# Batch 2 transposed in tile 0's second half, its global rows gathered by SyncE, its values loaded in fp32, and two key casts on ScalarE

## The chip, the cores and the metric

The kernel runs on one core of one Trainium2 chip. The metric is the device time of one execution in microseconds (us). Nine runs of the kernel before have a median of 350.7 us and lie between 349.97 and 352.67 us.

## What is computed

The reference is a sparse attention followed by a two-layer feed-forward stage. Cut to what matters:

```python
# q, k, v: 8 batches x 8 heads x 576 positions x 64, fp32; global_idx: 8 positions
scores = scale * np.matmul(q, k.transpose(0, 1, 3, 2))
mask = np.abs(pos[:, None] - pos[None, :]) <= 32
mask = mask | is_global[:, None] | is_global[None, :]
attn = softmax of scores where mask, else -1e9
x = (attn @ v).transpose(0, 2, 1, 3).reshape(4608, 512)
h = x @ w_in                                   # w_in 512 x 2048
g = np.maximum(h, 0.0) + np.log1p(np.exp(-np.abs(h)))
out = g @ w_out                                # w_out 2048 x 512
```

A query sees keys at most 32 positions away and the 8 global positions, and a global query sees everything.

## The kernel before

**The stages.** Batch 0's attention runs first, alone. Then come nine feed-forward tiles of 512 tokens, and the attention of batches 1 to 7 is threaded between their matmuls. A tile `n` has 16 slots. Slot `s` holds four matmuls of the first layer for tile `n` (`mm1`, L516 to L534), then the steps filed under `(16n+s, 0)`, then four matmuls of the second layer for tile `n-1` (`mm2`, L548, none in tile 0), then the steps filed under `(16n+s, 1)`. Each step is put there by `at(slot, half, function, arguments)` (L582), and `attend` (L666) calls what is filed. Nothing reorders the work afterwards: each engine runs its instructions in the order in which the program names them, and waits where an operand is not ready. Slots set only this order, not times, so an engine with little to do runs ahead of the slot that TensorE is in.

**Attention of one batch and one pair of heads.** Keys and queries must lie with the head dimension on the partitions. Batches 0 to 2 load runs of six positions (`load_runs`, L101), cast keys on an engine (`cast_runs`, L174), and turn both with TensorE transposes (`transposes`, L324) into a PSUM bank; `spread_columns` (L359) copies the bank into `KT` or `QT`. Batches 3 to 7 instead load whole token tiles (`load_tokens`), cast them on GpSimd (`cast_tokens`, L131), and are turned by a DMA transpose on SyncE's queue (`turn`, L135). Then `scores` makes two groups of products (L380) and their exponentials on ScalarE (L403), `mask` multiplies them by the band on VectorE (L412), `sums` and `values` multiply by ones and by the values (L434), `inv_ln` and `inv_exp` form the reciprocal on ScalarE (L456, L460), and `scale_x` writes the result into `xT` on VectorE (L472, L474). `glob_norm` and `glob_out` (L484, L490) do the global queries; `glob_out` is eight small GpSimd copies into `xT`. The first `mm1` of tile `n` waits for the batches that its tokens belong to.

**Columns of the global positions.** Batches 0 and 1 take them with six extra one-hot matmuls in `transposes` (L345). Batch 2 takes them in one go with `columns_of_2` (L496), 24 one-hot matmuls each for keys and queries, filed in slots 14 and 15 of tile 0. For batches 3 to 7, GpSimd issues 16 DMAs (`gather_rows`, L167), eight rows for keys and eight for queries, cast to bf16 on the way, in slots 18 to 25; `global_columns` (L504) transposes them in slot 27, and `spread_globals` (L142) copies them into each batch's tile.

**Batch 2 before.** Its transposes lie in tile 1: a key transpose of pair `p` at half slots 33, 39, 45, 51 and a query transpose half a slot later. GpSimd casts its keys and moves its queries into the key layout (`cast_runs` at slots 8 and 9), and loads its values with casting DMAs into `V1` (`load_v_cast`, L155, slot 12).

**PSUM.** During batch 0 and tile 0 one pool, `start_psum`, is open: two banks under tag `h`, which `mm1` alternates between, and three two-bank regions under tag `at`, handed out in turn to scores, sums, values and some transposes. At tile 1 this pool is closed and a second one opens over the same eight banks (L762 to L764): two banks `h`, one `o`, one `tp`, two regions `at`. The output of `mm2` takes `o`, and from its tile 1 on it alternates between `o` and `tp` (L554).

**Queues.** SyncE issues the loads of keys, of values and of batches 3 to 7, the DMA transposes and the stores; GpSimd issues the loads of queries, the weights and the gathers of rows. The loads of keys share the buffer `kq_f`, those of values share `v_f`, so a load waits for the casts of the one before. The framework numbers the DMAs of each of the two kinds over eight completion semaphores in turn: a DMA waits for the one eight places before it to have landed.

Of the kernel before, what the change touches and what calls it, by code (L numbers as in the profile page):

```python
# [19 lines left out]
P = 128  # L20
WIN = 32
KW = 120
NG = 8
# [17 lines left out]
def kernel(  # L41
# [43 lines left out]
    GB = B - 3  # L85
    glob_2 = {n: const.tile([P, NP, NG], BF16, name=f"{n}_g2") for n in "kq"}
# [31 lines left out]
    def tokens(n, b):  # L118
        if (n, b) not in tok:
            fresh = b < 5  # L120
            tok[n, b] = work.tile([P, NP * NTL * P], BF16, tag=f"{n}b", bufs=2, name=f"{n}t") if fresh else tok[n, b - 2]
            if fresh:
                nc.gpsimd.memset(tok[n, b][96:P], 0.0)  # L123
        return tok[n, b][:].rearrange("p (a t c) -> p a t c", a=NP, t=NTL)
# [17 lines left out]
    def spread_globals(n, b):  # L142
        dst = turned[n, b]
# [10 lines left out]

    def load_v_cast(b):  # L155
        o = V1[b % 2]
        nc.gpsimd.dma_start(out=o[KW:P], in_=v_rows[:, (b - 1) * HD:b * HD].unsqueeze(1).to_broadcast([NG, NTL, HD]))
        for t in range(NTL):
            nc.gpsimd.dma_start(out=o[:ST[t], t].rearrange("p (h d) -> p h d", d=D),  # L159
                                in_=v[b, :, KW * t:KW * t + ST[t], :].rearrange("h s d -> s h d"))  # L160

    def gather_v(g):
        nc.gpsimd.dma_start(out=v_rows[g:g + 1].rearrange("o (c d) -> c o d", d=D),
                            in_=v.rearrange("b h s d -> (b h) s d")[H:, bass.ds(positions[g], 1), :])


    def gather_rows(n, g):  # L167
        o = (hot_v[:].rearrange("p t c -> p (t c)") if n == "k" else VG[:])[g * GB:(g + 1) * GB, 0:HD]
        nc.gpsimd.dma_start(out=o.rearrange("p (h d) -> p h d", d=D).unsqueeze(2),
                            in_=src[n][B - GB:B, :, bass.ds(positions[g], 1), :])  # L170
# [68 lines left out]
    positions = []  # L239

    def load_positions():
        positions.extend(nc.values_load_multi_w_load_instructions(
            idx_r[0:1, :], engines=[mybir.EngineType.Pool], min_val=0, max_val=S - 1,
            skip_runtime_bounds_check_because="positions of the sequence")[1])
# [79 lines left out]
    def transposes(n, b, p, copy=nc.vector.tensor_copy, unread=0):  # L324

        parts = [(slice(0, P), lambda r: kqb[n, b][:, r, p * P:(p + 1) * P])]
        if n == "q" and b < 2:
            parts = [(slice(64 * e, 64 * e + 64), lambda r, e=e: raw[b][:, 2 * p + e, r * D:(r + 1) * D]) for e in range(2)]
        if b == 1 and p:
# [17 lines left out]
        else:  # L347
            copy = nc.vector.tensor_copy
            g = glob_2[n][:, p]
        spread = lambda: spread_columns(n, b, p, tb, g, copy)  # L350
        if b == 1 and p:
# [7 lines left out]
    def spread_columns(n, b, p, tb, g, copy):  # L359
# [5 lines left out]
        cg = copy if b < 2 else nc.gpsimd.tensor_copy  # L365
        if n == "k":
            cg(dst[:, p, :, KW:P], g.unsqueeze(1).to_broadcast([P, NTL, NG]))
        else:
            cg(dst[:, p, 0:4, KW:P], g.unsqueeze(1).to_broadcast([P, 4, NG]))
            cg(dst[:, p, 4, ST[4]:ST[4] + NG], g)  # L370
# [119 lines left out]
    def glob_out(b):  # L490
        xg = XG.pop(b)
        for g in range(NG):
            nc.gpsimd.tensor_copy(xT[:, :, b * S:(b + 1) * S][:, :, bass.ds(positions[g], 1)], xg[:, :, g:g + 1])  # L493


    def columns_of_2(n):  # L496
        ps = region("tp")
        for p in range(NP):
            for r in range(RUN):
                nc.tensor.matmul(out=ps[:, p * NG:(p + 1) * NG], lhsT=kqb[n, 2][:, r, p * P:(p + 1) * P],  # L500
                                 rhs=onehot[:NQ, r, :], start=(r == 0), stop=(r == RUN - 1))
        nc.vector.tensor_copy(glob_2[n][:].rearrange("p a g -> p (a g)"), ps[:, 0:NP * NG])

    def global_columns(n):  # L504
        rows = hot_v[:].rearrange("p t c -> p (t c)") if n == "k" else VG[:]
        ps = bank()
        tb = ps[:].bitcast(BF16)
        for p in range(NP):
            nc.tensor.transpose(out=tb[:, p * GB * NG:(p + 1) * GB * NG], in_=rows[:GB * NG, p * P:(p + 1) * P],
# [38 lines left out]
    def mm2(n, s):  # L548
        i, part = s // 4, s % 4
        if part == 0:  # L550


            last = n == n_tiles - 1
            ops[n] = psum["pool"].tile([P, d_model], FP32, tag="h" if last else "tp" if n and i % 2 else "o",  # L554
# [38 lines left out]
    for c in range(4):  # L593
        at(0, 0, load_w_out, c)
    for p in range(NP):
        for n in "kq":
            at(8 + p // 2, 0, cast_runs, n, 2, pair_heads(p), nc.gpsimd.tensor_copy)
    at(12, 0, load_v_cast, 2)
    for i, n in enumerate("kq"):
        at(14 + i, 0, columns_of_2, n)  # L600
        at(27, i, global_columns, n)
        for g in range(NG):
            at(18 + g, 0, gather_rows, n, g)

    def loads(b):
        s0 = STARTS[4 * b - 8] // 2
        if b == 3:
            k0, kt, q0, qt, v0 = s0 - 12, s0 - 7, s0 - 8, s0 - 3, s0 - 5
        elif b == 4:
            k0, kt, q0, qt, v0 = s0 - 15, s0 - 10, s0 - 11, s0 - 6, s0 - 8  # L610
        else:
            k0, kt, q0, qt, v0 = s0 - 23, s0 - 15, s0 - 16, s0 - 8, s0 - 9
        for n, first, last in (("k", k0, kt), ("q", q0, qt), ("v", v0, None)):
# [9 lines left out]
            else:  # L623
                at(last, 0, turn, n, b)
                at(max(last + 2, 28), 0, spread_globals, n, b)

    for b in range(1, B):
# [8 lines left out]
        for p in range(NP):  # L636
# [8 lines left out]
            if (b, p) != (1, 0):  # L645
                if b < 3:
                    step(to_transposes, transposes, "k", b, p)
                    step(to_transposes + (b > 1), transposes, "q", b, p)
# [9 lines left out]
            step(to_inverse, inv_exp, p)  # L658
            step(to_x, scale_x, b, p)
        step(to_x + (b > 1), glob_norm, b)  # L660
# [22 lines left out]
    load_positions()  # L683
# [6 lines left out]
    cast_runs("k", 0, pair_heads(2), nc.gpsimd.tensor_copy)  # L690
    build_mask_0(nc.vector)
    build_bias(0)
    cast_runs("k", 0, pair_heads(3), nc.gpsimd.tensor_copy)
# [8 lines left out]
    for i in range(NP):  # L702
        load_runs("k", 1, pair_heads(i))
    for grp in range(2):
        products(0, 0, grp)
    exponentials(0, 0, 0)
    transposes("k", 0, 1, unread=2)
# [95 lines left out]
```

The softmax here doesn't subtract the row's maximum and nothing guards it: scores larger than these inputs give would overflow.

## Time and profile before

| what | value |
|---|---|
| median of nine runs | 350.7 us |
| the profiled execution: time, span | 351.84 us, 350.2 us |
| TensorE busy (its matmuls) | 334.0 us, 95% of the span |
| ScalarE, VectorE, GpSimd busy | 270.3, 135.2, 128.1 us |
| clock granted to TensorE | 1.0 throughout |
| DMA, of which on SyncE's queue and on GpSimd's | 47.34 MB; 40.09 MB and 6.80 MB |

The span is what the hardware profiler saw from first to last instruction of the execution; 1.64 us of the measured time lie around it. In the page, each group of instructions has a line with its source line, engine, operation, output and inputs, count, busy time and mean duration, then the idle time of the engine just before and what ended it. L521 is `mm1`, L540 `mm2`. From the timeline: tile 0 begins at 31.66 us, its slot 10 at 54.03 us, tile 1 at 62.23 us, tile 2 at 106.75 us.

### The profile page before, as it was taken

Reading aid. Unit: us, or ns where it says so; the run is one execution under the profiler, and the core shown is the slowest. Engines: PE = TensorE matmul, PEld = TensorE weight load, DVE = VectorE, ACT = ScalarE, POOL = GpSimd, SP = SyncE. Lnnn points to the kernel's source line nnn. Section 1 sums busy time; section 2 is a strip of 40 time slices with the busy share of each in tenths; the row PEclk is TensorE's granted clock in tenths of the full one; section 3 lists DMA queues with packets and bytes.
Section 4 is the critical chain, followed back from the end, with each engine's and each line's share of the span. In section 5 each row is a group of like instructions: output and inputs, shape, how many; then the busy total and the mean of one; then the engine's idle time right before and its main releaser. Section 6 shows DMA issues by size and latency. Waiting matters only on the chain.

```text
span 350.2 us, 7185 instructions
## 1 busy us (share of the span) xinstructions
PE 334.0 (95%) x2757; PEld 162.8 (46%) x2757; DVE 135.2 (39%) x397; ACT 270.3 (77%) x425; POOL 128.1 (37%) x265
## 2 busy tenths in 40 slices
PE   7898898999799999999999999999999999999996
PEld 3555444444344444444444444444444444444444
DVE  7863362265543344333444443334333100100021
ACT  3677899788778988888888888888888777777700
POOL 7954648996476336315432451402000100000000
PEclk9999999999999999999999999999999999999999
DMA  7999999999996999999899888700000100010012
GB/s 168 212 231 210 206 188 195 179 149 199 170 214 141 167 196 177 220 188 223 184 180 185 175 187 154 127 32 30 32 30 32 62 30 32 30 60 32 30 60 90
DMA packets 128169, 47.34 MB, mean 135 GB/s; under 512 B 114288, under 2 KB 123416, under 8 KB 128136
## 3 DMA queue, kind: packets, MB, share of 16 engines
q1 hardware_dynamic: 113752, 40.09, 57.8%
q0 software_dynamic: 14240, 6.80, 14.6%
q8 instruction: 21, 0.34, 0.4%
q14 instruction: 12, 0.10, 0.1%
q10 hardware_dynamic: 144, 0.01, 0.0%
HBM read 37.56 MB, written 9.55 MB: 135 GB/s over the span
## 4 chain that ended last, share of the span: by engine, by line
PE 71%; DMA 10%; POOL 7%; issue 4%; ACT 2%; DVE 2%; SPq 1%; POOLq 0%; ACTq 0%
PE o L540 31%; PE hp L521 30%; PE av L434 5%; PE sc L392 3%; DMA kq_f<-in_k_dram 3%; DMA v_f<-in_v_dram 2%; DMA q_raw<-in_q_dram 2%; DMA hot_v<-in_k_dram 2%; DMA kq_f<-in_q_dram 1%; POOL kt L123 1%; SPq L140 1%; POOL kt L132 1%; ACT ex L403 1%; POOL V L159 1%; PE sc L385 1%
## 5 line engine op out<-in xcount | busy, mean ns | idle before, releaser
L521 PE MATMUL hp<-xT,w_in_t 128*128 128x512 bf16 x576 | 147.6, 380 | 2.7 <-POOL xT L493 1.4
L540 PE MATMUL o<-w_out_t,gt 128*128 128x512 bf16 (+1 forms) x592 | 145.3, 373 | 0.7 <-DVE ot L545 0.7
L533 ACT ACTIVATE e<-hp 128x512 f32<-128x512 f32 x128 | 76.2, 595 | 37.9 <-PE hp L521 36.5
L540 PEld LDWEIGHTS <-gt 128*128 128x128 bf16 x592 | 57.1, 98 | 66.0 <-issue 2.0
L534 ACT ACTIVATE gt<-e 128x512 bf16<-128x512 f32 x128 | 80.6, 630 | 4.1
L521 PEld LDWEIGHTS <-w_in_t 128*128 128x128 bf16 x576 | 52.2, 98 | 65.5 <-issue 5.8
L545 DVE COPY ot<-o 128x512 f32<-128x512 f32 (+1 forms) x37 | 24.9, 672 | 66.5 <-PE o L540 66.5
L403 ACT ACTIVATE ex<-sc 128x1008 bf16<-128x1008 f32 (+1 forms) x56 | 48.6, 919 | 1.7 <-PE sc L392 1.1
L412 DVE TENSOR_TENSOR ex<-ex,mask 128x1008 bf16<-128x1008 bf16 (+1 forms) x48 | 32.6, 684 | 20.9 <-ACT ex L403 19.8
L444 DVE TENSOR_REDUCE gs<-av 128x8 f32<-128x32 f32 x64 | 12.0, 187 | 60.9 <-ACT rz L456 57.5
L493 POOL COPY xT<-xg 128x4 bf16 x64 | 15.4, 241 | 54.4 <-DVE xg L488 51.0
L182 POOL CAST V<-v_f 128x512 bf16<-128x512 f32 (+3 forms) x45 | 23.2, 536 | 29.6 <-DMA v_f<-in_v_dram 23.9
L472 DVE TENSOR_TENSOR xT<-av,rz 128x480 bf16<-128x480 f32 x28 | 18.4, 657 | 37.2 <-ACT rz L460 37.0
L132 POOL CAST kt<-kq_f 120x512 bf16<-120x512 f32 (+1 forms) x25 | 16.2, 659 | 20.0 <-DMA kq_f<-in_k_dram 19.7
L456 ACT ACTIVATE rz<-av 128x616 f32<-128x616 f32 x28 | 19.0, 680 | 4.6 <-PE av L434 2.5
L132 POOL CAST qt<-kq_f 120x512 bf16<-120x512 f32 (+1 forms) x25 | 15.9, 645 | 14.8 <-DMA kq_f<-in_q_dram 14.7
L460 ACT ACTIVATE rz<-rz 128x616 f32<-128x616 f32 x28 | 19.7, 703 | 0.2
L434 PEld LDWEIGHTS <-ones 128*64 128x64 bf16 x384 | 12.5, 109 | 11.6 <-issue 11.2
L434 PE MATMUL av<-ex,ones 128*64 128x160 bf16 (+1 forms) x336 | 16.7, 233 | 0.8 <-DVE ex L412 0.8
L434 PE MATMUL av<-ex,V 128*64 128x160 bf16 (+1 forms) x336 | 16.2, 229 | 1.2 <-POOL V L182 1.2
L392 PE MATMUL sc<-QT,KT 64*128 64x200 bf16 (+2 forms) x200 | 13.4, 242 | 1.9 <-DVE xT L474 1.0
L434 PEld LDWEIGHTS <-V 128*64 128x64 bf16 x384 | 13.7, 110 | 2.2 <-POOL V L182 1.5
(137 smaller groups left out, 238.9 us busy)
## 6 DMA issues: line engine op xcount, KB each, us to landing
out_dram<-ot SPq DMA_DIRECT2D x35, 256.0 KB, 2.2
v_f<-in_v_dram SPq DMA_DIRECT2D x24, 240.0 KB, 6.3
kq_f<-in_k_dram SPq DMA_DIRECT2D x20, 240.0 KB, 5.1
kq_f<-in_q_dram SPq DMA_DIRECT2D x20, 240.0 KB, 4.8
kq_f<-in_k_dram SPq DMA_DIRECT2D x12, 288.0 KB, 8.5
w_in_t<-in_moe_w_in_dram POOLq DMA_DIRECT2D x4, 512.0 KB, 7.6
w_out_t<-in_moe_w_out_dram POOLq DMA_DIRECT2D x4, 512.0 KB, 16.0
v_f<-in_v_dram SPq DMA_DIRECT2D x6, 192.0 KB, 4.1
```

Source lines behind the costliest of these rows:

```text
L132: nc.gpsimd.tensor_copy(tokens(n, b)[:ST[t], :, t, :], kq_f[:ST[t], t * HD:(t + 1) * HD].rearrange("p (a c) -> p a c", a=NP))
L182: eng.tensor_copy(V1[b % 2][:rows, t, cols], v_f[:rows, t, cols])
L392: nc.tensor.matmul(out=sc[:, e, GOFF[t]:GOFF[t] + w], lhsT=kT[r, p, t, :], rhs=qT[r, p].rearrange("p t c -> p (t c)")[:, WLO[t]:WHI[t]], s ...
L403: nc.scalar.activation(out=ex, in_=sc[:, :, 0:GW[grp]], func=ACTF.Exp, scale=SCALE)
L412: nc.vector.tensor_tensor(out=ex, in0=ex, in1=masks[grp][:, 0:GW[grp]].unsqueeze(1).to_broadcast([P, 2, GW[grp]]), op=ALU.mult)
L434: nc.tensor.matmul(out=av[64 * e:64 * e + 64, OFF + lo:OFF + hi], lhsT=weight(t, e), rhs=exps[p, grp][rows, e, c:c + hi - lo], start=(firs ...
L460: nc.scalar.activation(out=RZ[p], in_=RZ[p], func=ACTF.Exp, scale=-1.0)
L521: nc.tensor.matmul(out=hp[:], lhsT=w_in_t[:, kd, kf * P:(kf + 1) * P], rhs=xT[:, kd, n * NT:(n + 1) * NT], start=(kd == 0), stop=(kd == KD ...
L533: nc.scalar.activation(out=e[:], in_=hp[:], func=ACTF.Exp)
L534: nc.scalar.activation(out=gts[n][:, kf, :], in_=e[:], func=ACTF.Ln, bias=1.0)
L540: nc.tensor.matmul(out=op, lhsT=gts[n][:, kf, i * P:(i + 1) * P], rhs=w_out_t[:, kf, cols], start=(kf == 0), stop=(kf == KF - 1))
L545: nc.vector.tensor_copy(ot[:, cols], op)
```

## The change

- **Batch 2's transposes** move from tile 1 to half slots 21, 24, 27 and 30 of tile 0. Keys and queries of a pair go together into one two-bank region. The queries are taken from their raw layout, twelve transposes of 64 columns instead of six of 128. The four moves of queries into the key layout are gone.
- **Global rows** are gathered for batches 2 to 7, by SyncE, in fp32, into two buffers that tile 0 does not use, and cast to bf16 by GpSimd in slot 6. `columns_of_2` and the small GpSimd copies of batch 2's columns are gone; `global_columns` runs in slot 10, `spread_globals` for batch 2 in slot 15. SyncE loads the eight positions into registers as well.
- **Batch 2's values** are loaded in fp32 on SyncE's queue (slot 9) and cast by GpSimd (slots 12 to 14).
- **Key casts of batch 0**, pairs 2 and 3, go from GpSimd to ScalarE, and the loads of batch 1's keys are named after them.
- **Batches 3 and 4** get fixed slots, mostly two slots earlier than before. The zeroing of their four token tiles goes from GpSimd to VectorE.
- **The second PSUM pool** has two single banks `o0` and `o1` for the output in place of `o` and `tp`.
- **`glob_norm`** of batch 0 and of batch 1 comes before the last `scale_x` instead of after it.

The diff, cut to its core:

```diff
-    GB = B - 3
-    glob_2 = {n: const.tile([P, NP, NG], BF16, name=f"{n}_g2") for n in "kq"}
+    GB = B - 2
...
             if fresh:
-                nc.gpsimd.memset(tok[n, b][96:P], 0.0)
+                nc.vector.memset(tok[n, b][96:P], 0.0)
...
     def gather_rows(n, g):
-        o = (hot_v[:].rearrange("p t c -> p (t c)") if n == "k" else VG[:])[g * GB:(g + 1) * GB, 0:HD]
-        nc.gpsimd.dma_start(out=o.rearrange("p (h d) -> p h d", d=D).unsqueeze(2),
-                            in_=src[n][B - GB:B, :, bass.ds(positions[g], 1), :])
+        if n not in g_f:
+            g_f[n] = work.tile([P, NT], FP32, tag="e", bufs=2, name="g_f")
+        nc.sync.dma_start(out=g_f[n][g * GB:(g + 1) * GB, 0:HD].rearrange("p (h d) -> p h d", d=D).unsqueeze(2),
+                          in_=src[n][B - GB:B, :, bass.ds(positions[SP][g], 1), :])
+
+    def global_rows(n):
+        return (hot_v[:].rearrange("p t c -> p (t c)") if n == "k" else VG[:])[:GB * NG, 0:HD]
+
+    def cast_rows(n):
+        nc.gpsimd.tensor_copy(global_rows(n), g_f[n][:GB * NG, 0:HD])
...
-        if n == "q" and b < 2:
+        if n == "q":
             parts = [(slice(64 * e, 64 * e + 64), lambda r, e=e: raw[b][:, 2 * p + e, r * D:(r + 1) * D]) for e in range(2)]
-        if b == 1 and p:
+        if (b, p) > (1, 0):
             if n == "k":
                 both[p] = region("tp")
...
-            ops[n] = psum["pool"].tile([P, d_model], FP32, tag="h" if last else "tp" if n and i % 2 else "o",
+            ops[n] = psum["pool"].tile([P, d_model], FP32, tag="h" if last else f"o{i % 2}",
...
-    for p in range(NP):
-        for n in "kq":
-            at(8 + p // 2, 0, cast_runs, n, 2, pair_heads(p), nc.gpsimd.tensor_copy)
-    at(12, 0, load_v_cast, 2)
-    for i, n in enumerate("kq"):
-        at(14 + i, 0, columns_of_2, n)
-        at(27, i, global_columns, n)
-        for g in range(NG):
-            at(18 + g, 0, gather_rows, n, g)
+    at(0, 0, load_positions, SP)
+    for i, n in enumerate("kq"):
+        for g in range(NG):
+            at(1 + 2 * i + g // 4, 0, gather_rows, n, g)
+        at(6, 0, cast_rows, n)
+        at(10, i, global_columns, n)
+        at(15, 1, spread_globals, n, 2)
+    for p in range(NP):
+        at(8, 0, cast_runs, "k", 2, pair_heads(p), nc.gpsimd.tensor_copy)
+        for n in "kq":
+            at((21 + 3 * p) // 2, (21 + 3 * p) % 2, transposes, n, 2, p)
+    at(9, 1, load_v_rows, 2)
+    at(9, 1, load_v, 2)
+    for t in range(NTL):
+        at(12 + t // 2, 0, cast_v, 2, t, nc.gpsimd)
...
-        if b == 3:
-            k0, kt, q0, qt, v0 = s0 - 12, s0 - 7, s0 - 8, s0 - 3, s0 - 5
-        elif b == 4:
-            k0, kt, q0, qt, v0 = s0 - 15, s0 - 10, s0 - 11, s0 - 6, s0 - 8
+        if b < 5:
+            k0, kt, q0, qt, v0 = ((14, 19, 18, 23, 22), (24, 29, 28, 33, 33))[b - 3]
...
-                at(max(last + 2, 28), 0, spread_globals, n, b)
+                at(first, 0, tokens, n, b)
+                at(last + 2, 0, spread_globals, n, b)
...
-                if b < 3:
+                if b < 2:
                     step(to_transposes, transposes, "k", b, p)
-                    step(to_transposes + (b > 1), transposes, "q", b, p)
+                    step(to_transposes, transposes, "q", b, p)
...
+            if (b, p) == (1, NP - 1):
+                step(to_x, glob_norm, b)
             step(to_x, scale_x, b, p)
-        step(to_x + (b > 1), glob_norm, b)
+        if b > 1:
+            step(to_x + 1, glob_norm, b)
...
-    cast_runs("k", 0, pair_heads(2), nc.gpsimd.tensor_copy)
     build_mask_0(nc.vector)
     build_bias(0)
-    cast_runs("k", 0, pair_heads(3), nc.gpsimd.tensor_copy)
...
     exponentials(0, 0, 0)
+    cast_runs("k", 0, pair_heads(2), act_copy)
...
     scores(0, 1, 0)
+    cast_runs("k", 0, pair_heads(3), act_copy)
+    for i in range(NP):
+        load_runs("k", 1, pair_heads(i))
...
-            psum.update(pool=ctx.enter_context(tc.tile_pool(name="psum", bufs=1, space=PSUM)), bank="tp", banks=1, at=2)
+            psum.update(pool=ctx.enter_context(tc.tile_pool(name="psum", bufs=1, space=PSUM)), at=2)
```

## The prediction

> **What bounds the kernel now.** I read the busy time by stretches first (columns: the stretch, its length, then busy us of TensorE's matmuls, its weight loads, VectorE, ScalarE and GpSimd, granted clock, DMA share, GB/s).
>
> ```profile
> 40.00:60.00 20.00, 18.73 (x240) 9.69 (x240) 8.27 (x36) 19.01 (x27) 13.29 (x26) 1.00 1.20 191
> 60.00:80.00 20.00, 18.66 (x188) 9.79 (x186) 8.91 (x22) 15.48 (x24) 19.79 (x31) 1.00 1.34 169
> 80.00:100.00 20.00, 17.45 (x167) 8.83 (x164) 10.52 (x32) 14.68 (x23) 11.25 (x25) 1.00 1.14 188
> ...
> 140.00:160.00 20.00, 20.00 (x154) 9.27 (x152) 8.01 (x21) 18.00 (x30) 5.92 (x11) 1.00 1.08 208
> ```
>
> From 140 us on TensorE has no idle time, so the end is what TensorE does plus its idle time before 140. Only the first 140 us can give or take. In tile 0 (31.66 to 62.23) ScalarE is nearly full; from 60 to 80 GpSimd is.
>
> Next the waits of TensorE's matmuls from 0 to 140 us (total us, times, longest):
>
> ```profile
> PE sc L392 <- DVE xT L474: 1.8, 3, 0.8
> ...
> PE hp L521 <- POOL xT L493: 1.4, 2, 0.8
> PE tp L509 <- DMA hot_v<-in_k_dram: 1.3, 1, 1.3
> PE av L434 <- POOL V L182: 1.2, 2, 0.7
> PE hp L521 <- ACT first_rz L527: 1.0, 2, 0.8
> PE av L434 <- DVE ex L412: 0.8, 2, 0.4
> PE o L540 <- DVE ot L545: 0.7, 1, 0.7
> ...
> PE hp L521 <- DVE q_g L502: 0.4, 1, 0.4
> ```
>
> The 14 waits add up to some 12 us. Those between 62 and 107 us (tile 1) are the three on `scale_x`, one on the mask, the gathered rows, the output copy, and 0.75 on `glob_out`.
>
> Last the timeline of tile 0's end: TensorE, ScalarE and VectorE.
>
> ```profile
> 54.03 1.90 PE L521 MATMUL hp<-xT,w_in_t 128*128 128x512 bf16 x8
> ...
> 56.71 1.89 PE L521 MATMUL hp<-xT,w_in_t 128*128 128x512 bf16 x8 [0.79 <-ACT first_rz L527]
> 58.78 1.02 PE L521 MATMUL hp<-xT,w_in_t 128*128 128x512 bf16 x4 [0.18 <-ACT first_rz L527]
> ...
> 61.10 0.75 PE L500 MATMUL tp<-onehot,qb 96*128 96x8 bf16 x24
> 62.23 0.59 PE L521 MATMUL hp<-xT,w_in_t 128*128 128x512 bf16 x2 [0.38 <-DVE q_g L502]
> ```
>
> ScalarE holds TensorE up by about 1 us there: the slack into which the transposes are put. The last row matters most: the first matmul of tile 1 waits for the copy of `q_g`, no operand of it. It is the first tile of the second PSUM pool, and waits until everything of the first has been read.
>
> **The Trainium skill.** "DMA: Bandwidth & Descriptors", section "SWDGE vs HWDGE vs iDMA": a DMA can cast only when GpSimd issues it. So moving loads to SyncE adds casts. The trace agrees: SyncE loads are fp32 with casts behind them. The same section has all DMAs share the same 16 engines, so a changed queue moves no byte away; the DMA share is above 0.9 until 120 us. "VectorE: DVE Perf Modes", section "Zero memsets can be issued as uint32 (trn2)": a zeroing of bf16 on VectorE can count half the elements. It agrees: 32x2560 bf16 took 2.23 us on GpSimd (L123), and the same size as 32x1280 uint32 1.12 us on VectorE (L209).
>
> **The change part by part.**
>
> *Before slot 10 of tile 0 (54.03 us).* The two key casts (0.83 us each on ScalarE) fall into its waits for TensorE, at 9.7 to 10.6 and 13.9 to 15.1; GpSimd's freed 1.6 us are mostly lost again, since its last `gather_v` waits for a query load until 13.09. The first `mm1` may come 0.1 us later through `glob_norm`. All this is covered by the wait for batch 1's values (0.52 and 0.67 us at 37.6 and 38.5), whose load lands at 38.03 behind a full DMA queue. I take 0, between -0.3 and +0.3.
>
> *Tile 0 from slot 10.* One `mm1` takes 0.87 us from start to start. Transposes of one pair take 0.42 (keys, 6) and 0.45 (queries, 12; rows at 42.03 and 42.51), hence 3.5 for four pairs; two `global_columns` 0.5. The two `columns_of_2` (1.4) go. With six `mm1` (5.3) that is 9.3 us of work where before 8.2 passed. Two waits come on top.
> (a) The regions are handed out in turn: keys' `global_columns` gets that of the last scores, queries' that of batch 1's last sums, and pair 0's transposes that of its last values. The last is free when `scale_x` has read it: 57.03 before, and 0.6 later (57.65) with `glob_norm` (0.34 and 0.28) put ahead. TensorE gets there at 55.1; queries' columns wait to 55.9 for `glob_sums`. So pair 0 starts at 57.7, and 2.4 us are lost less 0.2 of work between them. `mm1`, copies and ScalarE queue behind. From 57.7: two `mm1`, pair 1, one `mm1`, pair 2, two `mm1`, pair 3: about 3.4 + 4.4 less overlaps is 7.4, so 65.1. ScalarE keeps up: its 1.12 us per `mm1` now meet a slower TensorE.
> (b) VectorE copies each pair in four copies, 1.55 us (0.58 + 0.17 + 0.56 + 0.25 from start to start). It starts pair 0 at 58.15, after two `global_columns` copies, ends at 59.7; pair 1 runs 60.6 to 62.15, pair 2 62.2 to 63.75, the zeroing of batch 3's key tile (1.12) to 64.9, pair 3 to 66.4. The second pool opens then: tile 1 begins at 66.5 instead of 62.23, **+4.3 us**. Without both waits it is about +1.2.
>
> *Is the input there in time?* Row gathers are not on SyncE in this trace. GpSimd's rows landed 2.3 to 7.0 us after issue, median 4.9, and SyncE's stores in 2.2. SyncE is free from 35.6 to 46.2. Gathers 5 to 8 wait for batch 2's key loads to land (42 to 46 us), the second eight for the first. That puts the last landing at 53 to 55, the casts of rows (two, some 0.6 each) before 55.9, batch 2's four key casts (0.82 each) behind them on GpSimd from 55 to 58.5. TensorE needs the first at 57.7: no cost, with 1 to 2 us of margin. At 7.0 us per landing it is up to 4 us late. Moving values to SyncE (between gathers and batch 3's keys) costs TensorE nothing: needed after 70 us, landing near 62. They compete with `w_out_t`, which landed from 54.4 to 64.6; delayed 3 us, its last quarter is still ahead of its use at 72.
>
> *Tile 1 gives back.* Pair 0: both transposes gone, less a longer wait for the mask, 1.2 in all up to the end of its values. After values of a pair, the next pair's second scores come 3.85 us later in both cases, held by ScalarE's logarithm and exponential and by `scale_x` (72.48 to 76.33, 80.47 to 84.32): taking the query transpose out of this stretch only lengthens the wait. The key transpose lies outside: 0.35 each for pairs 2 and 3. At pair 3 the wait for gathered rows, 1.3, and `global_columns` go, but 3.85 from 88.45 hold scores until 92.3 instead of 93.2: 0.9. Up to batch 2's last values queries' columns (0.27), the output copy (0.73, now with a second bank) and a little more: 1.15. The 0.75 wait for `glob_out` ends: GpSimd was in a late cast until 104.3 while `xg` was ready at 102.9, and loses 16 gathers (9.0), six value DMAs (5.1), four zeroings (8.9), query moves (3.3) and small copies (2.6), against 5 value casts (3.2) and about 2 more. Sum 1.2 + 0.05 + 0.7 + 0.9 + 1.15 + 0.75 = **-4.75 us**, between -3.5 and -5.5. VectorE's other three zeroings fall between a mask and the next sums' logarithm: 0, at most 1.
>
> *After tile 2 begins* nothing on TensorE changes: 0.
>
> **Sum.** +4.3 - 4.75 = -0.45. The profiled execution took 351.84 us (span 350.2 and 1.64 around), which becomes 351.4. It lay 1.1 above the median of 350.7, which becomes **350.2**. Bounds: tile 0 +2.0 to +7.5, tile 1 as above.
>
> **Rivals.**
> *Faster: the waits in tile 0 don't add up.* If pair 0 doesn't wait for `scale_x`, or the pool opens earlier, tile 0 costs +1.2 to +2.5 and tile 1's gain stands: 347.2 to 348.4, say 348.0. For it: ScalarE held this stage, so lost TensorE time is partly free. Against: the wait on `q_g` shows that the pool waits for all of it.
> *Slower: late rows.* Eight SyncE DMAs in flight, each landing in up to 7 us behind 2 MB of `w_out_t`, make the second eight rows land at 60 rather than 54; batch 2's key casts are behind them on GpSimd, so are the transposes, the copies and the pool. It decides from about 1.5 us of lateness, then counts one to one: +4 us gives 354. For it: DMA share of 1.2 in this stretch. Against: SyncE's queue holds little else then.
> *The same, for another reason:* tile 1 gives only 3.5 and tile 0 costs 3.5; not told apart by time.
>
> **How the numbers follow.** About 0.3% (1.05 us) is what a measurement of this kernel can tell from no change. My forecast, near balance with 349.0 to 352.0, 0.42; faster 0.29; slower 0.29. Of the balanced case a part reaches past each bound, which makes faster 0.33, same 0.34, slower 0.33. The range, 347.2 to 354.2, takes in most of both rivals; the balanced case's own is 349.0 to 352.0.
>
> **What would show it.** Right: TensorE waits at slot 10 for `scale_x`, then at the first `mm1` of tile 1 for VectorE's copy into `QT`, tile 1 beginning near 66.5 and tile 2 near 106.3; waits for rows, output copy and `glob_out` gone, those for `scale_x` longer. Wrong: tile 1 begins before 65 (the faster case) or GpSimd's row cast waits for DMA past 57 (the slower). A first `mm1` of tile 0 moved by over 0.5 us, or idle time of TensorE after 140, would break the frame.

## The result and the profile after

The changed kernel takes 357.4 us (median of ten runs, 354.5 to 361.0); the kernel before took 350.9 beside it. The ratio is 1.0159, 95% interval 1.0130 to 1.0188: 1.6% slower. It compares mean times and leaves out the two slowest of the ten runs, 360.8 and 361.0 us. The forecast of 350.2 is wrong, and the range up to 354.2 doesn't hold the time. The profiled execution took 356.69 us, its span is 355.1, with a mean granted clock of 0.986. The runs of the changed kernel differ more among themselves than those of before, and the spans follow the clock roughly: 352.8 us at 0.998, 357.3 at 0.985, but also 356.3 at 0.994.

The stretches of the profile after, with the columns of the prediction's first fence:

```profile
40.00:60.00 20.00, 15.79 (x228) 8.71 (x226) 8.39 (x36) 15.19 (x21) 7.91 (x12) 0.91 1.23 197
60.00:80.00 20.00, 17.58 (x126) 7.98 (x123) 8.59 (x19) 11.91 (x18) 9.48 (x23) 0.83 1.06 163
80.00:100.00 20.00, 17.75 (x154) 8.39 (x153) 10.69 (x26) 16.77 (x27) 6.90 (x12) 1.00 1.12 202
...
140.00:160.00 20.00, 20.00 (x166) 9.63 (x164) 7.90 (x20) 17.83 (x30) 7.21 (x15) 1.00 1.01 194
```

Of the frame, one half holds: TensorE is full from 140 us on. The first `mm1` of tile 0 starts at 30.14 us, 1.5 earlier than before, which the forecast had named as a sign against it. But this start differs from profile to profile: in `b` to `h` below, which do the same work up to there, it lies between 30.25 and 32.08. So the text below compares lengths from slot 10 on, not starting times. The loss lies between 40 and 80 us, and the column that the prediction never used, the granted clock, has fallen there to 0.91 and 0.83. Finer stretches place it:

```profile
56.00:58.00 2.00, 0.00 (x0) 0.00 (x0) 0.84 (x3) 0.00 (x0) 0.61 (x2) 0.59 1.26 209
58.00:60.00 2.00, 1.51 (x22) 1.16 (x22) 0.26 (x1) 0.00 (x0) 2.00 (x3) 0.50 1.20 185
60.00:62.00 2.00, 2.00 (x9) 0.73 (x6) 1.55 (x4) 0.04 (x1) 1.82 (x6) 0.50 1.11 207
...
70.00:72.00 2.00, 1.52 (x4) 0.58 (x5) 0.34 (x2) 0.00 (x0) 1.51 (x6) 0.50 1.27 199
```

From 56 to 58 us TensorE does nothing at all, and then runs at half clock. It looks busy from 60 to 62 with 9 matmuls.

TensorE's waits from 0 to 140 us:

```profile
PE tp L501 <- POOL VG L170: 3.5, 1, 3.5
PE sc L393 <- DVE xT L475: 3.1, 4, 0.8
PE hp L513 <- POOL KT L145: 2.3, 1, 2.3
PE av L435 <- POOL V L182: 2.0, 2, 1.4
...
PE tp L341 <- POOL kb L177: 0.4, 1, 0.4
```

The gathered rows of tile 1, the output copy and the late wait for `glob_out` are gone, as forecast, and four waits for `scale_x` stand where three stood. Two are new: 3.5 us for GpSimd's cast of the query rows (L170), and 2.3 at the first `mm1` of tile 1. The 2.3 us are put down to a GpSimd copy (L145), but it is one of many things that the closing of the PSUM pool waits for. The timeline of TensorE shows both:

```profile
53.33 1.04 PE L513 MATMUL hp<-xT,w_in_t 128*128 128x512 bf16 x4
54.30 0.27 PE L501 MATMUL tp<-ident_bf,hot_v 48*128 48x48 bf16 x4
58.05 0.34 PE L501 MATMUL tp<-ident_bf,VG 48*128 48x48 bf16 x4 [3.48 <-POOL VG L170]
58.83 0.66 PE L341 MATMUL tp<-ident_bf,kb 96*128 96x96 bf16 x6 [0.43 <-POOL kb L177]
...
60.04 3.44 PE L513 MATMUL hp<-xT,w_in_t 128*128 128x512 bf16 x8
...
65.64 1.90 PE L513 MATMUL hp<-xT,w_in_t 128*128 128x512 bf16 x8
...
70.48 1.86 PE L513 MATMUL hp<-xT,w_in_t 128*128 128x512 bf16 x4 [2.31 <-POOL KT L145]
```

Eight matmuls of `mm1` took 3.44 us at 60.04 and 1.90 at 65.64: the same work at half and at full clock. GpSimd's and SyncE's timelines give the cause of the first wait:

```profile
49.85 0.61 POOL L170 CAST hot_v<-g_f 48x512 bf16<-48x512 f32 x1 [5.16 <-DMA g_f<-in_q_dram]
57.39 0.61 POOL L170 CAST VG<-g_f 48x512 bf16<-48x512 f32 x1 [6.93 <-DMA g_f<-in_q_dram]
57.95 3.13 POOL L177 CAST kb<-kq_f 96x768 bf16<-96x768 f32 x4
```

```profile
36.44 7.40 SPq L163 DMA_DIRECT2D g_f<-in_k_dram  x8
44.06 7.63 SPq L163 DMA_DIRECT2D g_f<-in_q_dram  x8
```

SyncE needs 0.95 us from one gather to the next, so the sixteenth leaves at 51.7; its row can be cast at 57.4, 5.7 us later. The key casts of batch 2 stand behind that cast in GpSimd's queue.

### The profile page after: what moved, and what is told of

Same layout as the page of the kernel before. It is cut to its first block, busy times and chain, and to the rows that moved or that the text cites. A ratio compares the mean times of both kernels' runs of the same rounds, so it can differ in the third digit from the quotient of the medians.

```text
span 355.1 us, 7138 instructions
## 1 busy us (share of the span) xinstructions
PE 335.8 (95%) x2733; PEld 162.4 (46%) x2733; DVE 136.2 (38%) x399; ACT 271.2 (76%) x427; POOL 103.8 (29%) x231
## 4 chain that ended last, share of the span: by engine, by line
PE 75%; DMA 8%; SPq 6%; ACT 5%; issue 2%; DVE 1%; POOL 1%; POOLq 0%; ACTq 0%
PE o L532 33%; PE hp L513 31%; PE av L435 6%; DMA v_f<-in_v_dram 4%; DMA kq_f<-in_k_dram 4%; SPq L163 4%; PE sc L393 4%; SPq L111 2%; ACT e L525 1%; ACT ex L404 1%; ACT gt L526 1%; DVE xT L473 1%; ACT rz L461 1%; ACT first_ex L404 0%; ACT kb L189 0%
## 5 line engine op out<-in xcount | busy, mean ns | idle before, releaser
L513 PE MATMUL hp<-xT,w_in_t 128*128 128x512 bf16 x576 | 150.2, 385 | 2.9 <-POOL KT L145 2.3
L532 PEld LDWEIGHTS <-gt 128*128 128x128 bf16 x592 | 57.4, 98 | 66.7 <-issue 2.1
L182 POOL CAST V<-v_f 128x512 bf16<-128x512 f32 (+3 forms) x50 | 26.1, 537 | 37.8 <-DMA v_f<-in_v_dram 30.1
L445 DVE TENSOR_REDUCE gs<-av 128x8 f32<-128x32 f32 x64 | 12.0, 188 | 61.1 <-ACT rz L457 56.7
L494 POOL COPY xT<-xg 128x4 bf16 x64 | 16.6, 260 | 57.9 <-DVE xg L489 53.9
L131 POOL CAST kt<-kq_f 120x512 bf16<-120x512 f32 (+1 forms) x25 | 15.3, 618 | 25.2 <-DMA kq_f<-in_k_dram 24.9
L461 ACT ACTIVATE rz<-rz 128x616 f32<-128x616 f32 x28 | 19.7, 703 | 0.2
L435 PE MATMUL av<-ex,V 128*64 128x160 bf16 (+1 forms) x336 | 16.1, 229 | 2.0 <-POOL V L182 2.0
L519 ACT ACTIVATE first_rz<-hp 128x512 f32<-128x512 f32 x16 | 9.5, 592 | 9.9 <-PE hp L513 9.6
```

The costliest lines, as they stand in the source:

```text
L131: nc.gpsimd.tensor_copy(tokens(n, b)[:ST[t], :, t, :], kq_f[:ST[t], t * HD:(t + 1) * HD].rearrange("p (a c) -> p a c", a=NP))
L182: eng.tensor_copy(V1[b % 2][:rows, t, cols], v_f[:rows, t, cols])
L435: nc.tensor.matmul(out=av[64 * e:64 * e + 64, OFF + lo:OFF + hi], lhsT=weight(t, e), rhs=exps[p, grp][rows, e, c:c + hi - lo], start=(firs ...
L461: nc.scalar.activation(out=RZ[p], in_=RZ[p], func=ACTF.Exp, scale=-1.0)
L513: nc.tensor.matmul(out=hp[:], lhsT=w_in_t[:, kd, kf * P:(kf + 1) * P], rhs=xT[:, kd, n * NT:(n + 1) * NT], start=(kd == 0), stop=(kd == KD ...
L532: nc.tensor.matmul(out=op, lhsT=gts[n][:, kf, i * P:(i + 1) * P], rhs=w_out_t[:, kf, cols], start=(kf == 0), stop=(kf == KF - 1))
```

## The experiments

All ratios are to the kernel before, run beside each. Each version was profiled in one execution, so the waits and clocks below are of that one. Fillers are matmuls of 512 columns (0.22 us each at full clock) whose result nobody reads.

**Four on where the loss lies.** `a_fill` adds 12 fillers ahead of the query rows' transposes and 9 at the end of tile 0:

```diff
+        for _ in range(12 if n == "q" else 0):
+            nc.tensor.matmul(out=ps[:, 0:512], lhsT=ident_bf[:], rhs=w_in_t[:, 0, 0:512], start=True, stop=True)
...
+    at(15, 1, hold, 9)
```

> The kernel after with unread matmuls in TensorE's two long waits (12 of 512 columns ahead of the queries' global columns, 9 ahead of the second PSUM pool); nothing else is moved. Theory 'late rows, and the clock that falls in the wait': the granted clock stays at 1.0 between 56 and 74 us, where it was 0.5 to 0.7, the matmuls after each wait take 0.22 us instead of 0.43, and about 3 us are won: 354.4, ratio to before 1.009. Rival 'the pool of PSUM and VectorE's copies': the clock costs nothing since VectorE sets the end of tile 0: 356.5 to 357.5, ratio 1.016.

355.8 us, ratio 1.0113 (1.0044 to 1.0182). The clock is 1.0 from 40 to 80 us, as the theory had it; the ratio lies between the 1.009 of the theory and the 1.016 of the rival. The rows and the key cast are still late: pair 0 comes 6.1 us after slot 10. From there to tile 1 it takes 9.6 us, 2.0 less than after, but then the first `mm1` of tile 2 waits 1.45 us for `glob_out`, which it didn't after. By the ratios the kept clock is worth about a quarter of the loss, though the intervals overlap.

`b_cols_late` moves only the transposes of the rows to slot 15; `c_rows_behind` also files the two row casts behind batch 2's key casts; `d_zero_pool` is `c` with the zeroing of the token tiles back on GpSimd:

```diff
-        at(10, i, global_columns, n)
-        at(15, 1, spread_globals, n, 2)
+        at(15, 1, global_columns, n)            # both columns, then both spreads
...
-        at(6, 0, cast_rows, n)
+        at(8, 0, cast_rows, n)                  # c, d: after the key casts
...
-                nc.vector.memset(tok[n, b][96:P], 0.0)
+                nc.gpsimd.memset(tok[n, b][96:P], 0.0)   # d
```

> The kernel after with both global_columns moved from slot 10 behind the last transposes (slot 15), GpSimd's order unchanged (casts of rows ahead of batch 2's key casts). Theory 'late rows hold GpSimd': the transposes of pair 0 still wait for the first key cast, which waits behind the rows, so pair 0 starts at 58 to 59 us as before and the time stays at 356 to 358, ratio 1.014 to 1.018. Rival 'the wait of the columns themselves on TensorE': pair 0 starts near 54.5 and the time falls to 351 to 352, ratio 1.002.

> As b_cols_late, and the casts of the rows also go behind batch 2's key casts on GpSimd. Theory 'late rows': pair 0 starts at 54.5, no wait over 1 us up to slot 15, the clock stays at 1.0, tile 1 begins near 65, and the time falls by 6 us to 351.4, ratio 1.000 (a wait for the columns or the values at slot 15 may keep 1 us of it). Rival 'PSUM pool and VectorE': VectorE's copies still end late and 354 to 356 remain, ratio 1.010. Rival 'values in fp32': GpSimd's value casts stay late at 64 to 70 and 356 to 357 remain.

> As c_rows_behind with the zeroing of the four token tiles back on GpSimd. Theory: the zeroing of batch 3's key tile (1.12 us on VectorE) lies between the copies of pairs 2 and 3, so tile 1 begins 0.5 to 1 us earlier than in c_rows_behind: 350.7, ratio 0.998. Rival: VectorE has time to spare at that place, and GpSimd's 2.2 us per zeroing delay the key casts of batch 3: no gain, or a loss of up to 1 us.

`b`: 1.0183 (1.0137 to 1.0229). TensorE no longer needs the rows in slot 10, yet waits 4.40 us there, now for the key cast behind them (`PE tp L341 <- POOL kb L177`). `c`: 1.0079 (1.0054 to 1.0105), the best version that computes the whole reference. Pair 0 is transposed at 54.6, and although GpSimd waits for the same rows until 58.1, nobody waits for GpSimd. So the lateness acted through GpSimd's order. Tile 1 begins at 65.0, as expected, yet the time is 2 us above what was expected, for this:

```profile
64.96 1.23 PE L513 MATMUL hp<-xT,w_in_t 128*128 128x512 bf16 x4 [2.51 <-DVE q_gT L503]
65.98 1.91 PE L532 MATMUL o<-w_out_t,gt 128*128 128x512 bf16 x4
```

The pool's wait is 2.5 us, and behind it the clock falls (1.91 for four matmuls that take 1.03). Beyond that, `glob_out` is waited for again, 1.05 us at tile 2. `d`: 1.0140 (1.0091 to 1.0190). The pool's wait is shorter, 1.77, but batch 2's scores wait 2.62 for GpSimd's copies of global columns. So giving the zeroing back to GpSimd gained nothing; it looks dearer there, though the intervals overlap.

**Four on the waits behind it.** `e_zero_early` is `c` with `at(8, 0, tokens, "k", 3)`, which zeroes batch 3's key tile before VectorE is busy; `f_hold` adds `at(15, 1, hold, 6)`.

> The kernel with the columns and row casts at slot 15.5 (c_rows_behind, ratio 1.0079), with the zeroing of batch 3's key tile moved from slot 14, where VectorE did it between pairs 2 and 3, to slot 8, where VectorE has little to do. Theory (the wait at tile 1's start is the end of VectorE's queue: zeroing 1.1 us, copies, columns' copies): the wait before the first product of tile 1 falls from 2.5 us to 1.4, tile 1 begins near 63.9 instead of 65.0; about 352.4 us, ratio 1.0045, and if the clock no longer falls after the shorter wait, 351, ratio 1.000. Rival (GpSimd's global outputs or key copies end last): wait stays 2.3 to 2.5, ratio 1.008.

> e_zero_early with six products that nobody reads (1.3 us at the full clock) behind the last transposes of tile 0, so that TensorE isn't idle while VectorE empties the old PSUM pool. Theory (the clock at tile 1's start falls because TensorE idles there): granted clock 1.0 from 60 to 80 us, tile 1's first four blocks at 0.95 us each, 1.5 us less than e_zero_early if that one still loses the clock: about 351, ratio 1.000. Rival (the fall has another cause, such as activity before 60): the fall to 0.6 stays and the time is that of e_zero_early, ratio 1.0045 or above.

`e`: 1.0100 (1.0053 to 1.0148). The pool's wait fell from 2.51 to 1.77, not to the 1.4 expected, the clock fell behind it all the same, and the median shows no gain. `f`: 1.0148 (1.0106 to 1.0189). The clock holds at the pool, but a wait comes two slots later:

```profile
68.60 1.27 POOL L182 CAST V<-v_f 128x512 bf16<-128x512 f32 x2 [1.19 <-DMA v_f<-in_v_dram]
69.81 0.39 POOL L145 COPY KT<-k_gT 128x160 bf16<-128x160 bf16 x1
70.14 0.35 POOL L147 COPY QT<-q_gT 128x128 bf16<-128x128 bf16 x1
```

GpSimd's copies of the global columns stand behind the casts of batch 2's values, whose fp32 loads are the next in SyncE's queue behind the sixteen gathers. TensorE waits 2.45 us for L147, and there the clock falls instead. My expectation had named nothing there.

`g_wout_late` issues the output weights behind the row casts; `h_values_cast` gives batch 2's values back to GpSimd's casting transfers:

```diff
-    for c in range(4):
-        at(0, 0, load_w_out, c)
...
         at(6, 0, cast_rows, n)
+        for c in range(2):
+            at(6, 0, load_w_out, 2 * i + c)
```

```diff
-    at(9, 1, load_v_rows, 2)
-    at(9, 1, load_v, 2)
-    for t in range(NTL):
-        at(12 + t // 2, 0, cast_v, 2, t, nc.gpsimd)
+    at(12, 0, load_v_cast, 2)
```

> The changed kernel with the four loads of the output weights (2 MB, issued by GpSimd at 41.7 to 44 us, landing 13 to 21 us later) put behind the casts of the global rows: two behind the key rows' cast, two behind the query rows' cast. Theory (the rows land late because they share 16 busy DMA engines with those loads): the query rows are cast by 54.5 instead of 58.0, TensorE's wait for them falls from 3.5 us to below 1, the clock stays full up to the pool's wait, tile 1 begins near 67, ratio 1.006 (353 us), unless the later weights hold mm2 up. Rival (the pace of SyncE's own sixteen issues, 0.93 us each, and their landing sets it): cast at 57 to 58 again, ratio 1.016.

> The changed kernel with batch 2's values loaded and cast by GpSimd's own transfers at slot 12, as in the kernel before: no fp32 loads on SyncE at slot 9.5, no ten casts on GpSimd in slots 12 to 14. Theory (the late rows and the clock made the loss, the values' way costs nothing): row wait 3.5 us and the clock's fall stay, ratio 1.016 within 0.003. Rival (GpSimd waits until 70 us for the fp32 values, and batch 2's key copies and batch 1's global outputs behind them hold up tile 1): the 2.3 us wait at tile 1's start falls to 1.4 or less, ratio 1.012 or below.

`g`: 1.0246 (1.0187 to 1.0306). The query rows are cast at 57.8, 5.9 us after the last issue, no sooner without the weights ahead of them, and the weights' issue now delays the key casts. This theory of mine fell: traffic of the weights isn't what makes the rows late. `h`: 1.0275 (1.0226 to 1.0324), above what I expected. Its profile has the same waits (3.5 for rows, 2.3 at the pool) and tile 1 as long as after. The rival, that the fp32 values make the pool's wait, is refuted; why the median is a per cent worse, the profile doesn't show.

**Four on the order and the engine of the gathers.** `i_spread_first` is `f` with the value casts at slots 16 to 18. `j_rows_gpsimd` lets GpSimd gather with casting DMAs, ahead of the output weights and behind batch 2's queries; `k_rows_hold` adds the early zeroing and the six fillers. `l_key_casts` puts the key casts of batch 0 and the loads behind them back as before.

```diff
-        at(12 + t // 2, 0, cast_v, 2, t, nc.gpsimd)
+        at(16 + t // 2, 0, cast_v, 2, t, nc.gpsimd)      # i
...
-        nc.sync.dma_start(out=g_f[n][...], in_=src[n][B - GB:B, :, bass.ds(positions[SP][g], 1), :])
+        nc.gpsimd.dma_start(out=o.rearrange(...).unsqueeze(2), in_=src[n][B - GB:B, :, bass.ds(positions[POOL][g], 1), :])   # j, k
```

> f_hold (ratio 1.0148) with the five casts of batch 2's values moved from slots 12 to 14 to slots 16 to 18, so that GpSimd copies batch 2's global columns ahead of them. Theory (in f_hold the copies of the columns stood behind casts that waited for fp32 values until 69.8 us, TensorE waited 2.4 us for them in tile 1 and lost its clock at 72): that wait goes, the clock stays at 1.0 through tile 1's start, 3.5 us less than f_hold: 351.5 to 352, ratio 1.003. Rival (the value casts then hold up the key casts of batch 3 and the global outputs, so the wait only moves to the values or to tile 2): less than 1.5 us gained, ratio 1.011 or above.

> The changed kernel with the global rows of batches 2 to 7 gathered by GpSimd's casting transfers, ahead of the output weights, instead of by SyncE with two casts on GpSimd; batch 2's queries are loaded first in tile 0 for it. Theory (SyncE's sixteen issues end at 51.7 and their rows land 5 to 6 us later, and that makes the 3.5 us wait and the clock's fall): no wait for rows in slot 10, the clock stays up to 66 us, tile 1 begins near 66, about 352.5 us, ratio 1.004. Rival (wherever they are gathered, something in slots 10 to 15 waits as long, for instance for key casts behind GpSimd's issues): tile 1 begins at 69 or later, ratio 1.012 or above.

> j_rows_gpsimd with the zeroing of batch 3's key tile at slot 8 and six products that nobody reads at the end of tile 0. Theory: the pool's wait 1.1 us shorter and no fall of the clock at tile 1's start, 2 to 2.5 us less than j_rows_gpsimd: 350, ratio 0.998, which would be the forecast of no change come true. Rival (the pool's wait or the clock doesn't depend on these): same as j_rows_gpsimd.

> The changed kernel with the two key casts of batch 0 back on GpSimd and the loads of batch 1's keys back where the kernel before has them. Theory (this part of the change lies beside other work): tile 0 begins at the same time, the rows still wait 3.5 us, ratio that of the changed kernel, 1.016 within 0.003. Rival (ScalarE's casts are on the path of the first scores): 1 us or more less, ratio 1.012 or below.

`i`: 1.0103 (1.0074 to 1.0133): the wait for L147 is gone, and in the profiled execution the clock is 1.0 throughout; in most of the other ten it was about 0.99. The 1.003 expected didn't come. `j`: 1.0231 (1.0156 to 1.0305) and `k`: 1.0228 (1.0155 to 1.0300): the times are those of the rivals, although in `k` the pool's wait and the clock's fall at tile 1 are gone from the profile. GpSimd's seventh and eighth gather wait for the weights `w_in_t` (4.5 us together in `j`, 6.2 in `k`), the last is issued at 57 to 58, and the key casts come behind. So GpSimd, at this place in its queue, gathers later than SyncE; another place was not tried. `l`: 1.0164 (1.0079 to 1.0249): no cost of that part shows, as forecast, to within 0.9%.

**Six on what the lateness is worth alone.** `m_rows_ready` leaves every step in place but casts the key rows twice, so that nothing needs the query rows; `n_rows_hold` adds the early zeroing and six fillers; `o_half_gathers` is `m` without the eight gathers of the query rows; `p_rows_first` issues all gathers ahead of batch 2's key loads; `q_rows_first_hold` is `p` with fillers (three and six in slot 10, six at slot 15), the early zeroing and late value casts; `r_forecast` is `o` with these fillers and the early zeroing.

```diff
-        nc.gpsimd.tensor_copy(global_rows(n), g_f[n][:GB * NG, 0:HD])
+        nc.gpsimd.tensor_copy(global_rows(n), g_f["k"][:GB * NG, 0:HD])   # m, n, o, r
...
+        at(4, 0, load_runs, "k", 2, pair_heads(p))      # p, q: moved here from the start
...
+        at(10, i, hold, 3 + 3 * i)                      # q, r
+    at(15, 1, hold, 6)                                  # n, q, r
```

> The changed kernel in which the second row cast reads the key rows, which are there by 50 us, instead of the query rows: all sixteen gathers are still issued, the query columns of batches 2 to 7 are wrong. Theory (the late landing of the query rows and the clock's fall after it are what my sum lacked): no wait in slot 10, pair 0 transposed at about 54.6, clock 1.0 from 52 to 66, tile 1 begins near 66 with the pool's wait of 2.3 us still ahead of it, perhaps with a lower clock for 4 us; 350.5 to 352, ratio 1.002 with 0.004 to either side. Rival (the loss is in the moved transposes and VectorE's copies, and the wait for rows only overlaps it): tile 1 begins at 68 or later, ratio 1.010 or above.

> m_rows_ready with the zeroing of batch 3's key tile at slot 8 and six products that nobody reads at the end of tile 0. Theory: the pool's wait falls by 1.1 us and the clock stays at 1.0 at tile 1's start; 1.5 to 2.5 us less than m_rows_ready, ratio 0.997. Rival (a wait for GpSimd's copies of the global columns behind the value casts takes their place, as in f_hold): no gain over m_rows_ready.

> m_rows_ready without the eight gathers of the query rows (they are not issued at all), so that SyncE's queue is 7.6 us shorter and batch 2's values are loaded from 44 us on instead of 52. Theory (SyncE's lateness costs by the rows alone): as m_rows_ready within 0.003. Rival (the values, and the copies behind their casts on GpSimd, are late because of the sixteen issues and cost tile 1 as well): 1 us or more less than m_rows_ready.

> The changed kernel with the four loads of batch 2's keys (4.8 us of SyncE's queue) put behind the sixteen gathers instead of ahead of them. Theory (the rows land 5 to 6 us behind their last issue, so they come with the issue): query rows cast by 53 instead of 58, no wait for rows; the waits for VectorE in slot 10 (0.7 and 1.3 us) that the row wait covered come in its place, pair 0 at slot 10 plus 3.5 us, as in m_rows_ready: ratio 1.010 within 0.004. Rival (batch 2's keys, later by 10 us or more, then hold pair 0 up as long as the rows did): ratio 1.016 or above.

> p_rows_first with nine products that nobody reads in slot 10 and six at the end of tile 0, the zeroing of batch 3's key tile at slot 8, and the value casts behind the copies of the global columns. Theory: the waits are those of my sum (3.5 us from slot 10 to pair 0, the pool's wait 1.2), the clock stays at 1.0, tile 2 begins 0 to 1 us after the kernel before: 350 to 352, ratio 1.000 with 0.004 to either side. Rival (a loss of about 1% stays whatever is done to rows and clock): ratio 1.008 or above.

> o_half_gathers (key rows cast twice, no gathers of the query rows, so the query columns of batches 2 to 7 are wrong) with nine products that nobody reads in slot 10, six at the end of tile 0, and the zeroing of batch 3's key tile at slot 8. Theory (late rows and the fallen clock are what the sum lacked): from slot 10 to pair 0 3.5 us, to tile 1 12.5 us, to tile 2 52.3 us, where the kernel before takes 52.7; the clock 1.0 from 48 to 100 us in most runs; 350 to 352, ratio 1.000 with 0.003 to either side. Rival (a loss remains that is neither rows nor clock, for instance ahead of slot 10): from slot 10 to tile 2 still 52.3, but the median at a ratio of 1.005 or above.

Ratios: `m` 1.0099 (1.0065 to 1.0134), `n` 1.0085 (1.0063 to 1.0107), `o` 1.0133 (1.0074 to 1.0192), `p` 1.0099 (1.0061 to 1.0137), `q` 1.0102 (1.0059 to 1.0145), `r` 1.0045 (1.0026 to 1.0065). Only `p` came as expected. The times of `m`, `n` and `q` are those of their rivals, `o` lies a little above both of its cases, and `r` between its two. In `o` TensorE's timeline is the one that the prediction described:

```profile
54.00 1.04 PE L513 MATMUL hp<-xT,w_in_t 128*128 128x512 bf16 x4
54.97 0.27 PE L501 MATMUL tp<-ident_bf,hot_v 48*128 48x48 bf16 x4
55.97 0.26 PE L501 MATMUL tp<-ident_bf,VG 48*128 48x48 bf16 x4 [0.73 <-DVE gs L445]
57.49 0.41 PE L341 MATMUL tp<-ident_bf,kb 96*128 96x96 bf16 x6 [1.26 <-DVE xT L475]
...
67.12 1.37 PE L513 MATMUL hp<-xT,w_in_t 128*128 128x512 bf16 x3 [2.30 <-DVE QT L364]
```

Queries' columns wait for `glob_sums` (L445) and pair 0 for `scale_x` (L475), both by name. `m` shows the same 0.73 and 1.26, and its clock falls there (0.59 from 58 to 60); in `o` it falls behind the pool's wait. `p` reaches slot 10 with real rows, by SyncE's order alone:

```profile
32.35 7.40 SPq L163 DMA_DIRECT2D g_f<-in_k_dram  x8
39.95 7.67 SPq L163 DMA_DIRECT2D g_f<-in_q_dram  x8
47.72 2.33 SPq L103 DMA_DIRECT2D kq_f<-in_k_dram  x4
```

The issues take the same 7.4 and 7.7 us although no key load is ahead of them. So the pace is SyncE's own, not a wait for the loads before. The last leaves at 47.6 and is cast at 52.9, 5.3 us later. There is no wait for rows then, but 1.70 us for `scale_x`, and the clock falls to 0.51 (58 to 60). In `q` the casts of values, moved back, hold the values' matmuls of tile 1 for 2.1 us in three waits, and the clock falls behind them, so it tells nothing of the rest.

`r` has the clock at 1.0 throughout its profile. The third row is the kernel before:

```profile
66.85 1.02 PE L513 MATMUL hp<-xT,w_in_t 128*128 128x512 bf16 x4 [0.34 <-DVE QT L364]
...
108.23 1.02 PE L513 MATMUL hp<-xT,w_in_t 128*128 128x512 bf16 x3 [1.30 <-POOL xT L494]
...
106.75 1.02 PE L521 MATMUL hp<-xT,w_in_t 128*128 128x512 bf16 x4 [0.75 <-POOL xT L493]
```

Tile 1 begins 12.53 us after slot 10 (54.32), and the forecast said 12.47; its six fillers of slot 15 fill what is left of the pool's wait. But 1.30 us go at the first `mm1` of tile 2, for `glob_out`, whose GpSimd timeline is:

```profile
104.67 1.53 POOL L131 CAST kt<-kq_f 120x512 bf16<-120x512 f32 x2 [0.78 <-DMA kq_f<-in_k_dram]
106.15 2.03 POOL L494 COPY xT<-xg 128x4 bf16 x8
```

`xg` was ready at 103.4; GpSimd was in key casts of batch 4, which waited for SyncE's loads. Ten of the 22 runs of `r` had a clock of 0.993 to 0.995. The other twelve, at 0.999 or 1.0, still have a median of 352.8, where runs of the kernel before at 0.998 or above have 350.8: most of what `r` loses is not the clock.

## Why the prediction was wrong

Times from the profiles, in us; ratios as given above. "Tile 1" is from its first `mm1` to that of tile 2.

| kernel | slot 10 at | to pair 0 | slot 10 to tile 1 | tile 1 | ratio |
|---|---|---|---|---|---|
| before | 54.03 | none | 8.20 | 44.52 | 1 |
| forecast | 54.03 | 3.67 | 12.47 | 39.77 | 0.999 |
| after | 53.33 | 5.50 | 17.15 | 41.17 | 1.0159 |
| `a`, fillers alone | 54.67 | 6.13 | 15.77 | 41.53 | 1.0113 |
| `m`, rows there | 54.92 | 3.49 | 14.65 | 40.30 | 1.0099 |
| `o`, and fewer gathers | 54.00 | 3.49 | 13.12 | 41.42 | 1.0133 |
| `p`, gathers first | 52.75 | 3.92 | 15.05 | 41.14 | 1.0099 |
| `r`, and fillers | 54.32 | 3.46 | 12.53 | 41.38 | 1.0045 |

The sum for the changed kernel against the forecast: tile 2 begins at 111.65 instead of 106.27, 5.4 us later. Of these, -0.7 are the earlier slot 10, 1.8 the later pair 0 (5.50 against 3.67), 2.85 the way from there to tile 1 (11.65 against 8.80), 1.4 tile 1 itself.

**"Is the input there in time?" is the step that failed.** It took SyncE as free and the landing as the term that counts, and concluded "no cost, with 1 to 2 us of margin". It left out the issue: it counted sixteen issues as 9.0 us of relief for GpSimd and charged SyncE nothing for them. Sixteen at 0.95 us make 15.2 us from 36.4, so the second eight can't all leave before 51.7. With a landing of 5.7 us that is 57.4; the step had 53 to 55. The prediction's own sign for the slower case, a row cast that waits past 57, is what came. Its mechanism wasn't: neither the eight in flight nor the weights set it (`p`, `g`). The bare wait for rows costs less than its 3.5 us, and not one to one as that rival had it, since 2.0 us of waits for `glob_sums` and `scale_x` lie under it; what is left, with the wait for the key cast, is the 1.8.

**The clock was missing from the sum.** A wait in the sum was priced at its length. After the 3.9 us in slot 10 pair 0 and eight matmuls took 2.0 us too long, after the pool's 2.3 the first two slots of tile 1 took 1.45 too long. That is 3.5 of the 5.4 us. Not all of it can be won back: in `a`, at full clock, tile 2 begins only 1.0 us sooner after slot 10, since pair 0 comes 0.6 later and `glob_out` waits 1.45. By the ratios, the rows in time take 1.0159 to 1.0099 (`m`), fillers, the early zeroing and half of the gathers left out take it to 1.0045 (`r`). The Trainium skill, "TensorE: Matmul & The Clock Gate", section "What's actually happening", says that the gate halves the clock after an idle window of about 3.4 us, and "HAM oscillation — how this bites in real kernels" warns of idle gaps above that. The 3.48 us of slot 10 agree; the falls behind 2.3 (after), 1.8 (`e`) and two waits of 0.7 and 1.3 (`m`) don't, and the measurement decides. That fillers take the falls out of the places where they stand (`a`, `f`, `r`) shows that idleness is their cause.

**Waits (a) and (b) in tile 0 were right.** (a), the regions: 3.49 with the rows there, 3.67 forecast. (b), VectorE's copies: from pair 0 to tile 1 9.63 us in `o` at full clock, 8.80 forecast: 0.8 too little. The early zeroing takes 0.7 off the pool's wait (`c` against `e`).

**"Tile 1 gives back" was right, with one term that depended on lateness.** After, less the 1.45 of the clock: 39.7, forecast 39.77; `o` less 1.7: 39.7. But the 0.75 for `glob_out` is gone only because tile 2 is late. In `r`, where tile 1 begins early, SyncE's loads and GpSimd's casts don't come earlier with it, and the wait is 1.30, more than before. The step had counted the work that GpSimd loses, not the loads that its casts wait for. So the forecast's balance was not had even with rows in time and the clock kept: `r` is 0.45% slower than before, 1.6 us, and this wait is 1.3 of the 1.7 us by which its tile 2 begins later after slot 10 than forecast.

Key casts on ScalarE, values by SyncE and zeroing on VectorE show no cost in the changed kernel (`l`, `h`) and in `c` (`d`), as forecast. Other waits lie over them, though: in `f`, with the pool's wait filled, the casts of the values do hold TensorE up, for 2.45 us. Not one of the 18 versions was faster than the kernel before.

**What stays open:** why the rows of a gather take 5 to 6 us to be there; when a wait of around 2 us costs the clock and when not; and why `o`, with fewer gathers than `m`, has no better median, though its profiled execution is 1.3 us shorter. Of its other runs there is no profile. Nor was a version tried in which `glob_out` comes in time, so that this wait is the rest of the loss is read from the profile of `r` alone.

## What to carry to other kernels

Moving small DMAs to an idle queue isn't free: count issues times the issue time of that engine, then add the landing of the last one, and compare with the first reader and with everything queued behind that reader. Price an idle stretch of TensorE of about 2 us and more at its length plus, as here, perhaps another 1.4 to 2.1 us for half clock, and look at the granted clock of each stretch in every profile. A wait that vanishes because the reader has become late comes back as soon as the reader is on time.

## What the runs showed of the hardware

- A gather of 12 KB cost SyncE 0.95 us, at the same rate whether or not key loads were ahead of it (after, `p`); GpSimd, waiting, could cast eight rows 5.2 (`p`) to 6.4 us (`c`) after the last of their issues.
- TensorE's clock was halved behind waits of 1.8 to 2.5 us in some profiles (`e`, after, `c`) and not behind 2.3 in `m` or 2.6 in `d`; one fall cost 1.4 to 2.1 us.
- Five loads of batch 2's values (52.3 us after, 50.8 in `p`, 44.8 in `o`) held SyncE's queue for 13.3, 16.1 and 19.7 us: started 7.5 us sooner, they ended 1.1 us sooner.
